# Routed attention and a squared-ReLU layer on one core: the last attention sums placed behind all remaining plain products

## The chip, the cores and the metric

The kernel runs on one core of a Trainium2 chip. The metric is the device time of one execution in microseconds (us); the figure for a kernel is the median of its runs. A profile is one further execution, recorded by the hardware profiler. The engines are called as the profile calls them: PE (TensorE matmuls), PEld (its weight loads), DVE (VectorE), ACT (ScalarE), POOL (GpSimd) and SP (SyncE, which issues most transfers here).

## What is computed

The reference has two halves. Attention with routing: queries and keys go to the nearest of 16 centroids, and a query sees only keys of its own cluster. Then a layer that squares its ReLU.

```python
# q, k, v: (4, 8, 768, 64); centroids: (8, 16, 64)
q_assign = argmax(q_n @ c_n)              # per head
k_assign = argmax(k_n @ c_n)
scores = (q @ k.T) / 8, or -1e9 where q_assign != k_assign
attn = softmax(scores);  attn_out = attn @ v
# x: (3072, 512), w_in: (512, 2048), w_out: (2048, 512)
x = attn_out, heads side by side
out = relu(x @ w_in) ** 2 @ w_out
```

## The kernel before

Attention runs in units: a pair of heads, a half of the queries, and two of six key chunks. The scores are exponentiated on ACT and masked on DVE. The products with v are summed on PE in a PSUM tile `av`. The sums for the softmax's denominator are first accumulated on POOL in `acc`, and then summed over partitions on PE (`sm`). `add_up` makes the reciprocal and sends it through DRAM to be spread over the partitions (`rb`); `finish` scales `av` with it into `xT`, the input of the second layer.

```python
def add_up(pair, h):                       # cut: the branch of the first pairs
    total = acc.pop((pair, h))
    sm = bank("sm", [P, TB // 2])
    one = [ones_products(sm, e, total[:, e], True, True) for e in range(2)]
    together([p for both in zip(*one) for p in both])      # four products on PE
    r = once.tile([P, TB // 2], F32, name="r")
    nc.vector.reciprocal(out=r, in_=sm)
    ...
    nc.sync.dma_start(far.rearrange("e (g n) -> (e g) n", g=2), r)
    for e in range(2):
        nc.sync.dma_start(rb[D * e : D * (e + 1)], far[e].partition_broadcast(D))
    nc.sync.dma_start(seen[row : row + 4], r)

def finish(pair, h):
    nc.vector.scalar_tensor_tensor(out=x, in0=av.pop((pair, h), x), scalar=UP,
        in1=spread_out.pop((pair, h)), op0=ALU.mult, op1=ALU.mult)
```

The second layer exists in two forms. The plain one, `ffn`, is used for the first of the four batches only. It is a generator whose products are dealt out among the attention units, so that PE has work where attention waits; `fill_steps(n)` takes the next products of it, up to n columns. `left[0]` is what remains of it, and the share of each unit is computed so that `RESERVE = 3 * DM` columns stay for the end.

```python
for u in range(len(units) + 3):
    ...                                    # scores, finish, products with v
    for pair, h in complete:
        with tc.high_priority(offset=1000) if first_half(pair, h) else ExitStack():
            add_up(pair, h)
    ...
    fill_steps(left[0] - goal)             # this unit's share of plain products
...
fill_steps(left[0])                        # what is left of them
ctx.close()                                # attention's buffers are given back
banks = fast.enter_context(tc.tile_pool(name="banks", bufs=8, space=PSUM, reuse_waits="tile"))
```

The other form, `ffn_pair`, does the remaining three batches after attention, with seven products of half size for eight (a Strassen-Winograd scheme). It needs sums of its inputs beforehand: of `xT` and of `w_out` on DVE (`x_t`, and `w_t` 1 to 4), of `w_in` on POOL (`w_s`). Its PSUM tiles, called `bank`, are eight, and lie where attention's PSUM tiles lay (`sc`, `av`, and `sm` with the others of its pool), so that a product into a bank waits for the last reader of what was there.

```python
def combine(c, product, width, early=()):  # cut
    product(1, bank); nc.scalar.copy(out=c11, in_=bank)
    add(6, (c12, c11)); add(2, (c11, c11)); add(7, (c21, c12))
    add(5, (c22, c21), (c12, c12)); sub(c21, c21, bank_of(4)); add(3, (c12, c12))

for i in range(F2):                        # first part of a batch, cut
    w_s = ...                              # s1..s4: four sums on POOL
    if i > 1 and w_sums:
        to, one, two = w_sums.pop(0)
        sub(w_t[to], one, two)             # sums of w_out on DVE
    combine(c, product, TB)                # products on PE, sums on DVE
```

The order of instructions on each engine is made by the scheduler from this program, its dependences and priorities.

Of the kernel before, what the change touches and what calls it, by code (L numbers as in the profile page):

```python
# [25 lines left out]
def kernel(  # L26
# [88 lines left out]
    def load_v(pair):  # L115
        b, hp = divmod(pair, HP)
        raw_v[pair] = loads_v.tile([P, 2, NCH, D], F32, name="v_raw")
        nc.sync.dma_start(
            raw_v[pair], v[b, 2 * hp : 2 * hp + 2].rearrange("h (p j) d -> p h j d", p=P)
        )  # L120
# [16 lines left out]
    def load_weights(i):  # L137
        raw_w[i] = wstage.tile([P, NW, 2], U32, name="w_raw")
        nc.sync.dma_start(raw_w[i], weights[i][1])
# [134 lines left out]
    def split_words(pair, which):  # L274
        if which == 0:
            words[pair] = dram.tile([2 * NCH, P, 2, 2 * D], U16, name="words")
        flat = loads.tile([P, NCH, 2, 2 * D], U16, name="flat", tag="qk")
        src = raw[pair][which].bitcast(U16).rearrange("p c (d two) -> p c two d", two=2)
        half = NCH // 2
        with tc.issue_after(last_exp[0]):  # L280
            for cols in (slice(0, half), slice(half, NCH)):
                nc.scalar.copy(out=flat[:, cols], in_=src[:, cols])
        nc.sync.dma_start(
            words[pair][NCH * which : NCH * (which + 1)].rearrange("c p two d -> p c two d"),
            flat,
        )
        if which == 1:
            raw.pop(pair)
            load_qk(pair + 1)
# [126 lines left out]
    def prep(pair):  # L416
        if pair < HP:
            return [
                lambda: turn(pair, 0), lambda: turn(pair, 1), lambda: turn(pair, 2),
                lambda: logits(pair), lambda: route(pair),  # L420
                lambda: turn_onehot(pair, 0), lambda: turn_onehot(pair, 1),
            ]

        split = [lambda i=i: split_words(pair + 1, i) for i in range(2 if pair + 1 < NG else 0)]
        first, second = split or (None, None)
        return [
            lambda: turn_words(pair), None, None, first, None, None,
            lambda: logits(pair), None, lambda: route(pair), second, None, None,
            None, None, lambda: spread(pair),
        ]  # L430
# [10 lines left out]
    def first_half(pair, h):  # L441
        return pair < HP and h == 0
# [62 lines left out]
    def times_v(pair, h, c):  # L505
        if c == 0:
            av[pair, h] = ps_av.tile([P, TB], F32, name="av", tag="av")
            if first_half(pair, h):
                sums[pair, h] = ps_av.tile([P, TB // 2], F32, name="sm", tag="av")
        t = ex.pop((pair, h, c))  # L510
        products = [
            dict(
                out=av[pair, h][D * e : D * (e + 1)], lhsT=raw_v[pair][:, e, c + i],
                rhs=t[:, 2 * i + e], start=(c + i == 0), stop=(c + i == NCH - 1),
            )
            for i in range(2) for e in range(2)
        ]
        if first_half(pair, h):
            for i in range(2):
                one = [  # L520
                    ones_products(
                        sums[pair, h], e, t[:, 2 * i + e], c + i == 0, c + i == NCH - 1
                    )
                    for e in range(2)
                ]
                products += [p for both in zip(*one) for p in both]
        together(products, 4000)
# [76 lines left out]
    def ffn_pair(pools, b):  # L604
# [114 lines left out]
    units = [  # L719
        (pair, h, c)  # L720
        for pairs, halves in [(range(HP), [0]), (range(HP), [1])]
        + [([pair], [0, 1]) for pair in range(HP, NG)]
        for pair in pairs for h in halves for c in range(0, NCH, 2)
    ]
# [3 lines left out]
    left = [len(PLAIN) * per_half]  # L728
# [11 lines left out]
    def fill_steps(columns):  # L740

        while fill and columns > 0:
            if (passed := next(fill[0], None)) is None:
                fill.pop(0)
            else:
                columns -= passed
                left[0] -= passed

    def behind_first(u, what=last_logits):
        return tc.issue_after(what[0]) if u == 0 else ExitStack()  # L750

    def next_pair(u):

        pair, h, c = units[u]
        if c == 0 and pair + 1 < NG and h == 0 and (pair + 1) not in qkT:
            if pair + 1 < HP or pair >= HP:
                return pair + 1
        if u == TWOS + 4:
            return HP
        return None  # L760
# [17 lines left out]
    def ends(halves):  # L778
        for pair, h in halves:
            b, hp = divmod(pair, HP)  # L780

            with tc.high_priority(offset=1000) if (pair, h) == (HP - 1, 0) else ExitStack():
                finish(pair, h)
            if hp == HP - 1 and (b, h) in PLAIN:
                fill.append(ffn(b, h))

    for u in range(len(units) + 3):
        if u < len(units):
            pair, h, c = units[u]
            if (p := next_pair(u)) is not None:  # L790
                ahead.extend(prep(p))
            if u in (TWOS, TWOS + 2):

                split_words(HP, int(u > TWOS))
            if c == 0 and u + 3 < len(units) and units[u + 3][0] not in raw_v:
                load_v(units[u + 3][0])

            with behind_first(u):
                scores(pair, h, c)

        ends(added)
        added.clear()
        if u < TWOS:
            ready = u - 1
        elif u == TWOS or u % 2 or u >= len(units):
            ready = u

        complete, late = late, []
        while v_next < min(ready, len(units)):
            pair, h, c = units[v_next]  # L810
            times_v(pair, h, c)
            v_next += 1
            if c == NCH - 2:
                (late if h and not HP * NCH <= u < len(units) else complete).append((pair, h))
        for pair, h in complete:
            with tc.high_priority(offset=1000) if first_half(pair, h) else ExitStack():
                add_up(pair, h)
            if h == 1:
                for d in (qkT, ids, qid):
                    d.pop(pair)  # L820
            if h == 1 or pair < HP:
                raw_v.pop(pair)
            added.append((pair, h))

        rounding += 4
        while rounding >= 3:
            rounding -= 3
            i = next(to_round, None)
            if i is not None:
                with tc.issue_after(last_exp[0]):  # L830
                    round_weights(i)
                if (i := next(loaded, None)) is not None:
                    load_weights(i)
            elif not later:
                early.close()
                for name, bufs in (("xT", 5), ("out", 2)):
                    later[name] = keep.enter_context(
                        tc.tile_pool(name=name + "_late", bufs=bufs, side="right",
                                     reuse_waits="tile")
                    )  # L840
        share = 0
        if u % 2 == 0 or not TWOS < u < len(units):
            n = 2 if TWOS < u < len(units) else 1
            share = max(0, left[0] - RESERVE) * sum(map(density, range(u, u + n)))
            share //= max(1, sum(map(density, range(u, ENDS))))
        goal = left[0] - share

        for i in range(3):
            if i == 2:
                fill_steps(share * 2 // 3)  # L850
            if ahead:
                with behind_first(u, masked if i else last_logits):
                    (ahead.pop(0) or int)()
        fill_steps(left[0] - goal)
# [235 lines left out]
```

## Time and profile before

| | |
|---|---|
| time, median of 3 runs | 976.93 us (975.26 to 977.56) |
| span of the profiled run | 979.1 us |
| DVE busy, 530 to 539 us | 7.18 of 9.00 us |
| PE busy, 530 to 539 us | 7.41 of 9.00 us |
| PE busy, 539 to 560 us | 21.00 of 21.00 us |
| PE busy, 560 to 974 us | 413.37 of 414.00 us |
| granted TensorE clock | 0.997 |

In the page, a row of digits cuts the span into 40 slices and gives the busy share of each in tenths. In the chain of waits, each line has a start, a duration and the instruction that the end of the run is traced back to. In the timeline a line has a start, a busy time, engine, line of the kernel, operation, output and inputs with shapes, the number of merged instructions, and in brackets how long the engine sat idle before it and which instruction ended that. Attention ends near 534 us; the rest of the span is the second layer of three batches. Plain products are called `po` in its second part; `bank` stands for the products of the last stage.

### The profile page before, as it was taken

Reading aid. Unit: us, or ns where it says so; the run is one execution under the profiler, and the core shown is the slowest. Engines: PE = TensorE matmul, PEld = TensorE weight load, DVE = VectorE, ACT = ScalarE, POOL = GpSimd, SP = SyncE. Lnnn points to the kernel's source line nnn. Section 1 sums busy time; section 2 is a strip of 40 time slices with the busy share of each in tenths; the row PEclk is TensorE's granted clock in tenths of the full one; section 3 lists DMA queues with packets and bytes.
Section 4 is the critical chain, followed back from the end, with each engine's and each line's share of the span. In section 5 each row is a group of like instructions: output and inputs, shape, how many; then the busy total and the mean of one; then the engine's idle time right before and its main releaser. Section 6 shows DMA issues by size and latency. Waiting matters only on the chain.

```text
span 979.1 us, 12064 instructions
## 1 busy us (share of the span) xinstructions
PE 959.3 (98%) x4479; PEld 552.6 (56%) x4479; DVE 563.5 (58%) x913; ACT 316.1 (32%) x511; POOL 381.1 (39%) x277
## 2 busy tenths in 40 slices
PE   8999999999999999999999999999999999999997
PEld 4544444433444444444343555888556888556886
DVE  4869666666566665665657966531556531656331
ACT  5887655444445555544331211000111000111000
POOL 1337766555656556565567431002231002231000
PEclk9999999999999999999999999999999999999999
DMA  9667671544545454452310000000000000000000
GB/s 249 187 198 201 195 196 51 127 116 107 136 110 138 118 125 113 108 142 67 82 42 12 20 1 0 12 25 27 3 1 1 22 22 21 1 1 0 22 22 25
DMA packets 127746, 74.54 MB, mean 76 GB/s; under 512 B 90944, under 2 KB 119104, under 8 KB 127680
## 3 DMA queue, kind: packets, MB, share of 16 engines
q1 hardware_dynamic: 125968, 73.26, 28.4%
q8 instruction: 38, 0.62, 0.3%
q10 hardware_dynamic: 1712, 0.43, 0.2%
q14 instruction: 28, 0.23, 0.1%
HBM read 48.27 MB, written 15.86 MB: 65 GB/s over the span
## 4 chain that ended last, share of the span: by engine, by line
PE 81%; issue 6%; DVE 4%; DMA 4%; POOL 3%; SPq 2%; ACT 0%; POOLq 0%; DVEq 0%; ACTq 0%
PE bank L701 22%; PE bank L670 22%; PE ph L578 7%; PE po L591 7%; PE sc L91 6%; PE sc L94 5%; PE av L91 5%; PE av L94 4%; POOL w_in L167 2%; DMA rb<-far_r 2%; PE sm L91 1%; DVE ex L478 1%; DVE w_raw L155 1%; PE lg L91 1%; DMA qid<-far 1%
## 5 line engine op out<-in xcount | busy, mean ns | idle before, releaser
L490 POOL TENSOR_TENSOR acc<-acc,ex 128x768 f32<-128x768 f32 x112 | 207.2, 1850 | 109.3 <-DVE ex L478 94.8
L478 DVE SCALAR_TENSOR_TENSOR ex<-qid,ids,sc 128x384 f32<-128x384 bf16 x288 | 157.8, 608 | 64.9 <-ACT sc L474 42.0
L474 ACT ACTIVATE sc<-sc 128x768 f32<-128x768 f32 x144 | 108.5, 792 | 160.9 <-PE sc L94 138.8
L94 PE MATMUL sc<-qkT 64*128 64x384 f32 x576 | 152.3, 503 | 0.8
L94 PE MATMUL av<-ex,v_raw 128*64 128x384 f32 x576 | 135.6, 491 | 0.0
L659 POOL TENSOR_TENSOR w_s<-w_in 128x256 f32<-128x256 f32 x24 | 18.2, 757 | 273.8 <-PE bank L701 162.0
L640 DVE TENSOR_TENSOR g<-bank,g 128x384 f32<-128x384 f32 x144 | 77.8, 556 | 79.0 <-PE bank L670 77.9
L578 PE MATMUL ph<-xT,w_in 128*128 128x384 f32 x256 | 93.0, 505 | 4.0 <-DVE r L545 2.3
L701 PE MATMUL bank<-w_out,g 128*128 128x256 f32 x432 | 95.2, 379 | 0.0
L591 PE MATMUL po<-w_out,gT 128*128 128x512 f32 x192 | 91.7, 609 | 0.0
L91 PE MATMUL sc<-qkT 64*128 64x384 f32 x192 | 87.1, 534 | 3.0 <-DVE ex L478 2.8
L701 PEld LDWEIGHTS bank<-w_out,g 128*128 128x128 f32 x432 | 82.1, 190 | 11.8
L640 DVE TENSOR_TENSOR osb<-bank,osb 128x256 f32<-128x256 f32 x54 | 22.1, 423 | 107.6 <-PE bank L701 102.2
L94 PEld LDWEIGHTS sc<-qkT 64*128 64x128 f32 x576 | 65.1, 186 | 27.9 <-issue 5.3
L91 PE MATMUL av<-ex,v_raw 128*64 128x384 f32 x192 | 80.4, 500 | 0.0
L488 POOL TENSOR_TENSOR acc<-ex 128x768 f32<-128x768 f32 x28 | 51.5, 1839 | 51.0 <-DVE ex L478 37.9
L578 PEld LDWEIGHTS ph<-xT,w_in 128*128 128x128 f32 x256 | 46.5, 192 | 43.6 <-issue 15.3
L670 PE MATMUL bank<-xT,w_in 128*128 128x384 f32 x192 | 69.9, 487 | 0.0
L670 PE MATMUL bank<-x_t,w_s 128*128 128x384 f32 x192 | 69.8, 486 | 0.0
L670 PE MATMUL bank<-xT,w_s 128*128 128x384 f32 x192 | 69.8, 486 | 0.0
L94 PEld LDWEIGHTS av<-ex,v_raw 128*64 128x64 f32 x576 | 49.5, 137 | 34.1 <-issue 34.0
L701 PE MATMUL bank<-w_t,g 128*128 128x256 f32 x288 | 65.1, 379 | 0.0
(127 smaller groups left out, 1224.5 us busy)
## 6 DMA issues: line engine op xcount, KB each, us to landing
words<-flat SPq DMA_DIRECT2D x24, 384.0 KB
w_raw<-in_moe_w_in_dram SPq DMA_DIRECT2D x16, 512.0 KB
w_raw<-in_moe_w_out_dram SPq DMA_DIRECT2D x16, 512.0 KB
v_raw<-in_v_dram SPq DMA_DIRECT2D x20, 384.0 KB
rb<-far_r SPq DMA_DIRECT2D x64, 96.0 KB
q_raw<-in_q_dram SPq DMA_DIRECT2D x31, 192.0 KB
k_raw<-in_k_dram SPq DMA_DIRECT2D x31, 192.0 KB
out_dram<-osb SPq DMA_DIRECT2D x23, 256.0 KB
```

Source lines behind the costliest of these rows:

```text
L91: last = nc.tensor.matmul(**next(products))
L94: last = nc.tensor.matmul(**product)
L167: nc.gpsimd.tensor_tensor(out=dst, in0=dst, in1=lo, op=ALU.add)
L474: last_exp[0] = nc.scalar.activation(out=t[:, 2 * i : 2 * i + 2] if pair < HP else src, in_=src, func=ACT.Exp, scale=SCALE).ins
L478: last_mask[0] = nc.vector.scalar_tensor_tensor(out=t[:, 2 * i + e], in0=qid[pair][1][:, h, e], scalar=ids[pair][:, ch % NB, 2 + ch // NB, ...
L488: nc.gpsimd.tensor_tensor(out=acc[pair, h], in0=t[:, 0:2], in1=t[:, 2:4], op=ALU.add)
L490: nc.gpsimd.tensor_tensor(out=acc[pair, h], in0=acc[pair, h], in1=t[:, 2 * i : 2 * i + 2], op=ALU.add)
L578: nc.tensor.matmul(ph, lhsT=w_in[:, kk, f * P : (f + 1) * P], rhs=xT[b, h][:, kk], start=(kk == 0), stop=(kk == KT - 1),)
L591: nc.tensor.matmul(po, lhsT=gT[f][:, i * P : (i + 1) * P], rhs=w_out[:, f], start=(f == 0), stop=(f == FT - 1),)
L640: nc.vector.tensor_tensor(out=out, in0=bank, in1=to, op=ALU.add)
L670: nc.tensor.matmul(bank, lhsT=operands[j][0][:, kk], rhs=operands[j][1][:, kk], start=(kk == 0), stop=(kk == H2 - 1),)
L701: nc.tensor.matmul(bank, lhsT=operands[j][0][:, f], rhs=operands[j][1][:, f], start=(f == 0), stop=(f == F2 - 1),)
```

## The change

One call is added in the loop over units. In the last two passes, after all units have been recorded (`u > len(units)`), all plain products that are left are recorded ahead of `add_up`, in place of after it. The aim is that PE has all seven of them to do while POOL still accumulates what the last sums need.

```diff
             if c == NCH - 2:
                 (late if h and not HP * NCH <= u < len(units) else complete).append((pair, h))
+        if u > len(units):
+
+            fill_steps(left[0])
         for pair, h in complete:
             with tc.high_priority(offset=1000) if first_half(pair, h) else ExitStack():
                 add_up(pair, h)
```

The order of the built program differs from there on as follows, engine by engine. PE: `po` x2, `sm` x4, `po` x5 becomes `po` x7, `sm` x4. DVE: the reciprocal, which stood before the first of the four sums of `w_out`, now stands after it; the `xT` of the last half head, which stood after the first of these sums, now stands after the fourth. SP: the output of the last plain product is issued ahead of the reciprocal's transfers, in place of behind them. POOL and ACT keep their order.

## The prediction

> **What bounds the kernel now.** I read the busy shares first, then the chain that ended last, then the timeline around 530 us, where the diff acts. The page's shares and slices:
>
> ```profile
> PE 959.3 (98%) x4479; PEld 552.6 (56%) x4479; DVE 563.5 (58%) x913; ACT 316.1 (32%) x511; POOL 381.1 (39%) x277
> ...
> PE   8999999999999999999999999999999999999997
> ```
>
> TensorE (PE) is busy 98% of the span, so time can change only where PE idles, or comes to idle. The end of the chain, from the trace:
>
> ```profile
> 528.83 2.39 POOL acc L490
> 531.22 0.04 issue
> 531.26 0.02 POOLq L659
> 531.28 0.02 issue
> 531.30 2.41 POOL acc L490
> 533.71 0.04 issue
> 533.75 0.35 PE sm L91
> ...
> 534.28 4.49 PE po L591 x10
> 538.77 72.24 PE bank L670 x224
> ```
>
> From 538.77 on PE works through the three last-stage blocks without a hole; the chain leaves it only for the tail at 973. So whatever the first of these products gains or loses is carried to the end, about one for one. The only PE hole near the diff is ahead of the last sums:
>
> ```profile
> 530.18 1.98 PE L591 MATMUL po<-w_out,gT 128*128 128x512 f32 x4
> 533.75 0.35 PE L91 MATMUL sm<-acc,ups 128*32 128x192 f32 x1 [1.59 <-POOL acc L490]
> ...
> 534.21 4.56 PE L591 MATMUL po<-w_out,gT 128*128 128x512 f32 x10
> 538.61 1.45 PE L670 MATMUL bank<-xT,w_in 128*128 128x384 f32 x4
> ```
>
> A float32 product leaves two records, so x4 is two plain products and x10 the other five. PE has only two to do while GpSimd (POOL) finishes its accumulation; 1.59 us are lost. VectorE (DVE) around it:
>
> ```profile
> 535.83 1.34 DVE L545 RECIPROCAL r<-sm 128x192 f32<-128x192 f32 x1
> ...
> 540.06 2.80 DVE L612 TENSOR_TENSOR w_t<-w_out 128x2048 f32<-128x2048 f32 x1
> 542.79 0.55 DVE L564 SCALAR_TENSOR_TENSOR xT<-av,rb 128x384 f32<-128x384 f32 x1
> 543.26 2.28 DVE L612 TENSOR_TENSOR w_t<-w_out,w_t 128x2048 f32<-128x2048 f32 x1
> 545.46 2.28 DVE L612 TENSOR_TENSOR w_t<-w_out 128x2048 f32<-128x2048 f32 x1
> ```
>
> The reader is to see the order: reciprocal, one weight sum, xT, then the other weight sums. The order decides the case.
>
> **What the Trainium skill says.** (1) "PSUM — Partial Sum Buffer", section "Engine vs sequencer instructions": the VectorE, ScalarE and GpSimd queues are strict first-in-first-out, and matmuls start in program order. So an instruction that stands behind a waiting one waits too. The trace agrees: the seven plain products depend on nothing from POOL, and five of them stand behind the sums until 533.75. (2) "SBUF — State Buffer", section "SBUF: two separate sides": a DVE operation with two SBUF inputs and a GpSimd operation that reads SBUF take one shared port pair in turn, each for its whole instruction. The trace agrees: at 548.12 a weight sum starts while a POOL operation of 0.72 us from 547.88 is under way, and shows 2.63 us in place of 2.28; the POOL operation queued behind it from 548.57 shows 2.78 us. From 529 to 537 the subtractions of DVE and the operations of POOL alternate one for one in this way.
>
> **The change part by part.** It adds no instruction and removes none: `fill_steps(left[0])` records all remaining plain products ahead of `add_up` of the last half head. [...] What moves on DVE follows from the scheduler. Before: subtractions, reciprocal, check of sums, w_t1, xT, w_t2, w_t3, first g sum, w_t4. After: subtractions, **w_t1, reciprocal, w_t2, w_t3, w_t4, xT**, check of sums, g sums.
>
> Two waits of the new program decide what this costs. The second bank product needs the PSUM bank of the last sums, so it waits for the reciprocal that reads them. The seventh needs the bank of the last av, so it waits for xT. Both waits are in the old program too, but were over when PE came (reciprocal at 537.17 against a product at 539.90; xT at 543.34 against 546.35).
>
> Now in steps, in times of this trace.
> - PE, gain. The seven products run through: 532.16, the end of the first two, plus 5 x 0.854 (two records of 0.427) is 536.43. GpSimd's accumulation is over by 533.7, so the sums follow without waiting, and the first bank product starts at 538.61 - 1.59 = 537.02. **-1.59.**
> - DVE, w_t1. In the built program it waits for the last plain product, so it can't start before 536.43. POOL's operation of 0.73 us from 536.46 has the port, until 537.15. A free weight sum takes 2.20 from start to start (543.26 to 545.46): end 539.3.
> - Reciprocal, 1.36 (its rows give 1.345 to 1.359): end 540.65, where it ended at 537.17.
> - The second bank product was due at 537.02 + 1.29 = 538.31. It starts at 540.7: **+2.4.**
> - w_t2, w_t3, w_t4: three times 2.20, and POOL has three of its eight early operations (0.7 each) still to do, taking the port between them: 540.65 + 6.6 + two such waits of 0.7 is 548.65. xT, with one operand in PSUM, adds 0.5: 549.1. Its data is there: rb landed some 5.2 us after the reciprocal in the occurrence before (520.85 to 526.03), which is 545.9 here.
> - The seventh product is due five products after the second, 540.7 + 5 x 1.29 = 547.15, and starts at 549.15: **+2.0.**
> - Sum: -1.59 + 2.4 + 2.0 = **+2.8 us.** After that I find no further wait. The first ScalarE copy also waits for xT and ends near 549.7; the check of sums and the g sums follow on DVE, the first bank is free before the ninth product (551.7), and later ones come free faster than PE takes them: ten operations of some 0.55 in 9.03 us of PE.
>
> If the port is free whenever DVE wants it, the same sum gives: reciprocal at 540.05, second product +1.8, xT at 547.15, seventh product +0.65, in all +0.85. The alternation seen from 529 to 537 speaks for the longer one.
>
> **The rivals.**
> 1. *The plain reading:* the hole is filled and nothing else happens, -1.6 us, about 975.3. For it: the hole is on the chain, and PE is full behind it. Against it: w_t1 now stands ahead of the reciprocal and three sums ahead of xT, and the PE waits name those two.
> 2. *Only the bank of the sums counts:* the seventh product finds xT done, since w_t2 to w_t4 run undisturbed or the weight sums are shorter than I take them. -1.59 + 2.4, about +0.8: 977.7.
> 3. *The transfer is the bound:* far_r, then rb, start 3.5 us later and share the queue with the 256 KB output of the plain product. If rb took 8.5 us in place of 5.2, xT would wait for it and the loss would grow past 2.8. The DMA share is near 0 there, which speaks against it.
> 4. *Hidden:* the stall is made up by slack later. Against it: PE shows 413.37 us busy of 414 from 560 to 974.
>
> **Range and chances.** The mechanism gives +0.85 to +2.8, and I lean to the upper part: +2.6 on 976.93 is 979.5. The runs of the kernel before spread by 2.3 us, so I take about 1.6 to either side: 977.9 to 981.1. A 2% change is 19.5 us; the whole transition, from the hole to the last weight sum, is about that long, so nothing here can reach it. Within 2%: 0.98; each other side 0.01.
>
> **What would show it.** In the changed profile: po x14 without a hole ahead of the sums, first bank product near 537.0; reciprocal ending near 540.6, with w_t directly ahead of it; PE waiting some 2.4 us at the second bank product for DVE r, and some 2 us at the seventh for DVE xT; all later products some 2 to 3 us later than before. If PE shows no wait at these two, rival 1 holds and the kernel is faster by 1.6. If only the first shows, rival 2. If DVE idles ahead of xT for rb, rival 3.

## The result, and the profile after

The changed kernel took 980.84 us (median of 6 runs, 979.16 to 982.31), the kernel before 976.72 beside it: a ratio of 1.0039, 95% interval 1.002 to 1.0058. A later comparison of the same two kernels gave 981.87 against 979.26, a ratio of 1.003 (1.0015 to 1.0045). The change makes the kernel slower by some 0.3%: it fills the hole of 1.59 us ahead of the last sums, and opens two behind them, of 2.35 and 1.39 us.

On the page of the changed kernel the shares look as before:

```profile
PE 958.0 (98%) x4479; PEld 551.6 (56%) x4479; DVE 564.2 (58%) x913; ACT 316.0 (32%) x511; POOL 387.0 (39%) x277
```

The difference lies in 20 us of the timeline. Shown are its lines of PE (start, busy time, engine, line, operation, count, and in brackets the idle time before it and what ended it):

```profile
528.57 6.28 PE L591 MATMUL po<-w_out,gT 128*128 128x512 f32 x14
...
535.24 1.56 PE L670 MATMUL bank<-xT,w_in 128*128 128x384 f32 x4
...
539.14 1.53 PE L670 MATMUL bank<-x_t,w_s 128*128 128x384 f32 x4 [2.35 <-DVE r L545]
...
544.38 1.45 PE L670 MATMUL bank<-x_t,w_in 128*128 128x384 f32 x4
...
547.22 1.53 PE L670 MATMUL bank<-xT,w_s 128*128 128x384 f32 x4 [1.39 <-POOL w_s L612]
548.58 1.45 PE L670 MATMUL bank<-xT,w_in 128*128 128x384 f32 x4
```

All fourteen records of the plain products run through, and the 1.59 us ahead of the sums are gone. The second bank product waits for the reciprocal, and the seventh waits too. DVE and POOL in the same stretch:

```profile
534.88 2.85 DVE L612 TENSOR_TENSOR w_t<-w_out 128x2048 f32<-128x2048 f32 x1 [0.57 <-PE po L591]
...
537.65 1.34 DVE L545 RECIPROCAL r<-sm 128x192 f32<-128x192 f32 x1
...
538.92 2.22 DVE L612 TENSOR_TENSOR w_t<-w_out,w_t 128x2048 f32<-128x2048 f32 x1
538.96 2.77 POOL L612 TENSOR_TENSOR w_s<-w_s,w_in 128x256 f32<-128x256 f32 x1
...
541.07 2.81 DVE L612 TENSOR_TENSOR w_t<-w_out 128x2048 f32<-128x2048 f32 x1
541.69 2.77 POOL L612 TENSOR_TENSOR w_s<-w_in 128x256 f32<-128x256 f32 x1
543.80 2.81 DVE L612 TENSOR_TENSOR w_t<-w_t,w_out 128x2048 f32<-128x2048 f32 x1
544.42 2.77 POOL L612 TENSOR_TENSOR w_s<-w_in,w_s 128x256 f32<-128x256 f32 x1
546.53 0.55 DVE L564 SCALAR_TENSOR_TENSOR xT<-av,rb 128x384 f32<-128x384 f32 x1
```

The weight sum w_t1 stands ahead of the reciprocal, the other three ahead of xT. DVE works without a pause from 534.88 until xT is done, and the two PE waits end 0.15 us behind the end of the reciprocal (538.99) and 0.14 us behind that of xT (547.08). For the second of them the profile names a POOL sum, which ends at 547.19; the experiments settle which of the two it was. Behind that nothing gives the time back. In the chain that ended last, PE is again one block to the end:

```profile
547.22 64.74 PE bank L670 x200
611.96 72.52 PE bank L701 x336
684.48 0.12 PE every L869 x2
684.60 72.44 PE bank L670 x224
```

Since attention starts and ends at slightly different times from run to run, I compare **stretches** within one profile, both from the start of the plain products behind the last av: A to the start of the eighth bank product, B to the product of the check of sums (`every`). The two ends in the kernel before, from its timeline and its chain:

```profile
547.64 1.45 PE L670 MATMUL bank<-xT,w_in 128*128 128x384 f32 x4
...
683.53 0.12 PE every L866 x2
```

Before: A is 547.64 - 530.18 = 17.46, B is 683.53 - 530.18 = 153.35. After: A is 20.01, B is 684.48 - 528.57 = 155.91. So the profile shows +2.56 us from the transition.

### The profile page after: what moved, and what is told of

It reads as the page before. It is cut to its first block, busy times and chain, and to the rows that moved or that the text cites. A ratio compares the mean times of both kernels' runs of the same rounds, so it can differ in the third digit from the quotient of the medians.

```text
span 980.0 us, 12063 instructions
## 1 busy us (share of the span) xinstructions
PE 958.0 (98%) x4479; PEld 551.6 (56%) x4479; DVE 564.2 (58%) x913; ACT 316.0 (32%) x511; POOL 387.0 (39%) x277
## 4 chain that ended last, share of the span: by engine, by line
PE 86%; DVE 4%; DMA 3%; ACT 2%; issue 2%; POOL 2%; SPq 1%; ACTq 0%; DVEq 0%; POOLq 0%
PE bank L701 22%; PE bank L670 21%; PE po L591 7%; PE ph L578 7%; PE sc L91 7%; PE sc L94 6%; PE av L91 6%; PE av L94 5%; PE sm L91 1%; DMA rb<-far_r 1%; DVE w_raw L155 1%; PE lg L91 1%; POOL w_s L612 1%; ACT ex L474 1%; DVE ex L478 1%
## 5 line engine op out<-in xcount | busy, mean ns | idle before, releaser
L659 POOL TENSOR_TENSOR w_s<-w_in 128x256 f32<-128x256 f32 x24 | 20.2, 841 | 270.5 <-PE bank L701 162.0
```

Source lines behind the costliest of these rows:

```text
L659: nc.gpsimd.tensor_tensor(out=s1, in0=a[1][0], in1=a[1][1], op=ALU.add)
```

## The experiments

My theory: the loss is DVE's order. Rivals: plain products ahead of the sums cost by themselves, or through their output's transfer, which is now issued ahead of the reciprocal's (rival B); the seventh product waits for the POOL sum that the profile names, not for xT (rival C). In the table, the ratio with its interval compares the runs of both kernels and is not the quotient of the two medians; for `four` it is 0.9998, the quotient 0.9986.

| kernel | A, us | B, us | median beside before's, us | ratio (95%) |
|---|---|---|---|---|
| before | 17.46 | 153.35 | | |
| changed | 20.01 | 155.91 | 980.84 / 976.72 | 1.0039 (1.002 to 1.0058) |
| again | 20.01 | 155.90 | 981.87 / 979.26 | 1.003 (1.0015 to 1.0045) |
| four | 15.80 | 152.77 | 977.93 / 979.26 | 0.9998 (0.9985 to 1.001) |
| both | 16.60 | 156.62 | 980.62 / 979.26 | 1.0016 (1.0004 to 1.0029) |
| sm_av | 20.02 | 157.60 | 984.84 / 979.26 | 1.0067 (1.0047 to 1.0087) |
| four_late | 15.80 | 151.69 | 977.63 / 978.84 | 0.9985 (0.9976 to 0.9995) |
| seven_late | 16.13 | 152.02 | 977.07 / 978.84 | 0.9988 (0.9974 to 1.0002) |

**Four products ahead (four).** The edit against the changed kernel:

```diff
-        if u > len(units):
+        if u == len(units) + 1:
-            fill_steps(left[0])
+            fill_steps(2 * DM)
```

> Two plain products more ahead of the last sums (four, then three behind them), in place of all seven. I measure a stretch in the profile, from the start of the plain products behind the last av to the start of the eighth bank product: 17.46 us before (530.18 to 547.64), 20.01 in the changed kernel (528.57 to 548.58). Theory A (the loss is the order on DVE: reciprocal behind w_t1, xT behind w_t2 to w_t4): here the last plain product ends behind the sums, w_t1 cannot pass the reciprocal, PE waits nowhere, and the stretch is 17.46 - 1.59 = about 15.9; time about 975.1. Rival B (the loss comes from plain products as such ahead of the sums, or from their output's transfer ahead of the reciprocal's): a part of the loss stays, stretch above 17.

A was 15.80, as expected: no wait in it. B was only 0.58 below the kernel before, not 1.6, and the times don't separate the two. The list of what PE waited for from 540 us on has one line, with the total, the count and the longest:

```profile
PE bank L670 <- DVE g L640: 0.8, 1, 0.8
```

So there is a third place where DVE's backlog bites: the sums into g also stand behind w_t, and here the tenth product waits for the first of them to free its bank. Stretch A alone misses that.

**Both reorderings (both).** Against the changed kernel; the lines that keep the reciprocal and the last xT in `last_r` and `last_x` are left out:

```diff
-                sub(w_t[to], one, two)
+                with tc.issue_after(last_r[0]) if to == 1 else tc.issue_after(last_x[0]): sub(w_t[to], one, two)
```

> All seven products ahead, as in the changed kernel, but on DVE w_t1 is held behind the reciprocal and w_t2 to w_t4 behind xT. Theory A: the wait of the second bank product goes from 2.35 us to near 0.15; xT follows its transfer, some 5.2 us behind the reciprocal, and in the built program it is the sixth product that waits for xT, for some 0.6; stretch about 16.5, time about 975.7. Rival B (transfer order): the transfer of rb takes longer than 6 us, the stretch stays near 20.

A was 16.60 against 16.5 expected, with the wait of the second product gone. The time was a miss: I expected some 1 us less than the kernel before (975.7 against 976.72), and it took 1.4 us more than the one beside it (980.62 against 979.26). PE and DVE of this kernel:

```profile
541.78 1.56 PE L670 MATMUL bank<-x_t,w_in 128*128 128x384 f32 x4 [0.21 <-DVE xT L564]
...
549.38 2.40 PE L670 MATMUL bank<-xT,w_in 128*128 128x384 f32 x4 [2.17 <-DVE g L640]
551.58 2.34 PE L670 MATMUL bank<-xT,w_s 128*128 128x384 f32 x4
```

```profile
541.17 0.56 DVE L564 SCALAR_TENSOR_TENSOR xT<-av,rb 128x384 f32<-128x384 f32 x1 [1.97 <-DMA rb<-far_r]
541.64 2.28 DVE L612 TENSOR_TENSOR w_t<-w_out,w_t 128x2048 f32<-128x2048 f32 x1
...
546.04 2.82 DVE L612 TENSOR_TENSOR w_t<-w_t,w_out 128x2048 f32<-128x2048 f32 x1
548.78 2.80 DVE L640 TENSOR_TENSOR g<-bank,g 128x384 f32<-128x384 f32 x5
```

The three sums that I put behind xT now lie ahead of the first g sum, which starts at 548.78, and PE, at the tenth product, stands for 2.17 us. The wait was moved, not removed. Of the 3.27 us that B is above the kernel before, 1.80 are another thing: the tenth and eleventh products took 2.20 and 2.18 us from start to start in place of 1.29, at a granted clock of 0.50. The profiled execution took 981.98 us, more than the median, so how often the clock falls here isn't shown.

**The last sums in another bank (sm_av).**

```diff
-            sm = bank("sm", [P, TB // 2])
+            sm = (ps_av.tile(..., name="sm", tag="av") if (pair, h) == (NG - 1, 1) else bank(...))
```

> As the changed kernel, but the last sums lie in the other PSUM buffer of av, so that the second bank product no longer takes the bank that the reciprocal reads. Order on all engines unchanged. If the two waits simply add (2.6 and 1.6 of them), the stretch falls from 20.01 to 17.4. Theory A in its sharper form: both waits hang on one chain of DVE, whose end is xT; the second product's wait vanishes, and the seventh's grows from some 1.5 to some 4.1, since xT ends where it did; stretch again 20.0, time as the changed kernel. Rival C (the seventh product waits for the POOL sum that the profile names): the same start of the seventh product, so this run doesn't tell that apart.

A was 20.02, as the sharper form expected: the first wait vanished and the second grew from 1.39 to 3.97 us. PE in a second profile of it:

```profile
536.16 1.45 PE L670 MATMUL bank<-x_t,w_s 128*128 128x384 f32 x4
...
546.74 2.89 PE L670 MATMUL bank<-xT,w_s 128*128 128x384 f32 x4 [3.97 <-POOL w_s L612]
549.43 1.82 PE L670 MATMUL bank<-xT,w_in 128*128 128x384 f32 x4
551.09 1.45 PE L670 MATMUL bank<-x_t,w_s 128*128 128x384 f32 x4
```

This shows that the second product waits because of the bank, and that in the changed kernel the end of xT alone sets stretch A; taking the first wait away buys nothing. The time was not the changed kernel's, but 3 us above again's. B, 1.69 above the changed kernel's, shows part of it: behind the long wait a product takes 2.7 us (546.74 to 549.43) in place of 1.29, at a granted clock of 0.50.

**The changed kernel again (again).**

> The changed kernel once more, unaltered, for the size of the loss beside the others of this call: theory A gives +2.5 us over the kernel before (stretch 20.0), where the first comparison gave +4.1 with an interval of 2.0 to 5.7. If +4 stands, some 1.5 us lie outside the stretch.

+2.6 us by the medians, and A and B to within 0.01 of the first profile.

**The weight sums later (four_late and seven_late).** Both hold each sum of w_out behind the last squaring on DVE of the group before, with four plain products ahead of the sums or all seven. The line that keeps the squaring in `squared` is left out:

```diff
-                sub(w_t[to], one, two)
+                with tc.issue_after(squared[0]): sub(w_t[to], one, two)
```

> Four plain products ahead of the sums and three behind, and the four sums of w_out on DVE held behind the first, second, third and fourth groups of bank products (they are needed some 70 us later). The runs so far showed that the stretch to the eighth product isn't all: where it was short, PE waited once more behind it, for the first g sums, which stand behind w_t on DVE. So I now measure from the start of the plain products behind the last av to the product of the check of sums: 153.35 us before, 155.91 in the changed kernel, 152.77 with four ahead alone, 156.62 with both reorderings. Theory A, amended: DVE's backlog of the w_t sums is the cause of all three waits. Then no wait is left here: 153.35 - 1.66 = 151.7, time about 1.6 us under the kernel before. If something else delays the g sums (the transfer of rb, xT), a wait of 0.5 us or more stays.

> The changed kernel with all seven plain products ahead, and only the w_t sums held back as in the run before this. Amended theory A: the change by itself gains; the second product waits some 0.3 us for the reciprocal, which follows the sums at once, and nothing else waits: 152.0, time about 1.3 us under the kernel before. Rival B (plain products ahead of the sums, or their output's transfer ahead of the reciprocal's, cost by themselves): 154 or more.

B was 151.69 and 152.02, and PE's list of waits behind 540 us is empty in both. In the kernel with all seven ahead, DVE reads:

```profile
533.05 1.36 DVE L545 RECIPROCAL r<-sm 128x192 f32<-128x192 f32 x1 [1.07 <-PE sm L94]
...
539.74 0.56 DVE L564 SCALAR_TENSOR_TENSOR xT<-av,rb 128x384 f32<-128x384 f32 x1 [2.72 <-DMA rb<-far_r]
540.97 2.81 DVE L640 TENSOR_TENSOR g<-bank,g 128x384 f32<-128x384 f32 x5 [0.67 <-ACT g L644]
```

With the weight sums out of the way, all seven products ahead give a B 1.33 us below the kernel before, and 3.89 below the changed kernel. That refutes rival B: the plain products are all ahead, and their output's transfer goes first here too; from the end of the reciprocal (534.41) to xT are 5.3 us, as between an earlier pair in the kernel before (5.2 us, 520.85 to 526.03). The kernel before with only its sums held back wasn't run; its PE has no wait behind the sums (21.00 us busy of 21.00 from 539 to 560), which leaves nothing there to gain. In the times, seven_late isn't separated from the kernel before (its interval contains 1). Four_late has the shorter B, and its interval lies below 1: it is 0.15% faster than the kernel before.

**POOL's sums held back (pool_late, three profiles).** A copy of two elements of xT on POOL stands ahead of the four sums for the second group. Of the edit only the copy is shown; the sums are ordered behind it:

```diff
+ behind = nc.gpsimd.tensor_copy(out=..., in_=xT[B - 1, 1][:, KT - 1, 0:2]).ins   # for (b, i) == (1, 1)
```

> The changed kernel, but the four POOL sums for the second group of bank products are held back by a copy of two elements that reads xT. Port theory: in the changed kernel the second and third of w_t2 to w_t4 show 2.81 us for 2.2 because POOL sums lie between them; without these, each takes 2.2 to 2.3, xT ends 1.1 us earlier, and the eighth product starts 18.9 us behind the first plain product in place of 20.0. If the seventh product waits for the POOL sum that the profile names in front of it (w_s, which now ends some 3 us behind xT), its start moves back to 21.5 or later instead. If DVE's durations don't depend on POOL, nothing moves: 20.0.

> The kernel with the held POOL sums once more, unaltered. Its first profile showed xT done 17.45 us behind the first plain product, against 18.51 in the changed kernel, but the eighth product at 20.1: behind the wait of 2.36 us for the reciprocal the granted clock stood at 0.50 for some 3.4 us, and two products took 2.13 and 2.22 us for 1.29. Clock theory: the drop depends on how the wait falls in time, not on the kernel. If it stays away here, the eighth product starts at 18.9. If the slow products come from the held POOL sums, they are there again at full clock.

> The same again, for one more drawing: 18.9 at full clock, or 20.1 with a drop to 0.50 behind the wait.

A was 20.10, 18.95 and 19.98, B 155.99, 154.84 and 155.88. Each is one execution, so its time isn't compared. The second profile had full clock in this stretch; DVE and PE in it:

```profile
538.03 2.22 DVE L612 TENSOR_TENSOR w_t<-w_out,w_t 128x2048 f32<-128x2048 f32 x1
540.18 2.27 DVE L612 TENSOR_TENSOR w_t<-w_out 128x2048 f32<-128x2048 f32 x1
542.37 2.28 DVE L612 TENSOR_TENSOR w_t<-w_t,w_out 128x2048 f32<-128x2048 f32 x1
```

```profile
545.26 1.53 PE L670 MATMUL bank<-xT,w_s 128*128 128x384 f32 x4 [0.32 <-DVE xT L564]
546.63 1.45 PE L670 MATMUL bank<-xT,w_in 128*128 128x384 f32 x4
```

The second and third of these sums take 2.27 and 2.28 us in place of 2.81, xT ends 1.1 us earlier, and the seventh product follows xT. So POOL's sums between them, which the prediction puts down to the shared port, cost 1.06 us of the loss (20.01 to 18.95). And rival C falls: the POOL sum that stood in brackets is now behind xT, and the product doesn't wait for it; in the changed kernel it ended 0.11 us behind xT. The other two profiles lost the gain to the clock. In the lines of the third, each stretch has the busy time of PE, PEld, DVE, ACT and POOL, and at the end the granted clock, the DMA share and GB/s:

```profile
535.00:536.00 1.00, 0.69 (x1) 0.50 (x2) 1.00 (x2) 0.00 (x0) 0.00 (x0) 0.56 0.00 0
536.00:537.00 1.00, 1.00 (x3) 0.61 (x2) 1.00 (x1) 0.00 (x0) 0.00 (x0) 0.50 0.02 5
537.00:538.00 1.00, 1.00 (x2) 0.40 (x2) 1.00 (x2) 0.00 (x0) 0.00 (x0) 0.50 0.00 1
538.00:539.00 1.00, 1.00 (x4) 0.61 (x3) 1.00 (x1) 0.00 (x0) 0.00 (x0) 0.73 0.54 126
```

**Two more profiles, for the clock (sm_av_2, again_2).**

> The kernel with the last sums in the buffer of av once more. There the two waits are one of 3.97 us, and the first profile showed the clock at 0.50 for some 3.4 us behind it. Clock theory: a longer wait is followed by the drop more often than one of 2.35 us; I expect it again, and the product of the check of sums near 157.6 us behind the first plain product. Without the drop: 155.9.

> The changed kernel a third time. In two profiles the clock stayed at 1.00 behind its waits (2.35 and 1.39 us) and the product of the check of sums stood at 155.9. If the drop can follow these too, it shows here with some luck, and adds 1.7.

B was 157.59 in sm_av_2, again with the clock at 0.50 behind the wait, and 155.89 in again_2, again without that.

## Why the prediction was right

The time fell inside the range, the direction was right, and the waits came where the text put them. In us behind the first plain product:

| step | predicted | measured |
|---|---|---|
| first bank product | 6.84 | 6.67 |
| end of the reciprocal | 10.47 | 10.42 |
| second bank product | 10.52 | 10.57 |
| end of xT | 18.92 | 18.51 |
| seventh bank product | 18.97 | 18.65 |
| sum against the kernel before | +2.8 | +2.56 |

- Gain: -1.76 in place of -1.59. The first wait delayed the second product by 2.61 in place of 2.4, the second wait the seventh by 1.63 in place of 2.0. These misses partly cancel, so the sum is closer than its terms.
- Port: I took two waits of 0.7 between w_t2 and w_t4; they were 0.59 each (2.81 against 2.22). pool_late shows that they are POOL's doing, and the alternation seen from 529 to 537 was the right guide.
- Rivals 1 to 3 fall: both waits are there, DVE doesn't idle ahead of xT for rb, and the seventh product waits for xT as foretold, although the profile names a POOL sum; pool_late settled that. Rival 4 falls too: PE shows 414.00 us busy of 414 from 560 to 974.
- "After that I find no further wait" holds for the changed kernel, but only because PE is late anyway. In `four` and `both` the g sums behind w_t make a wait of their own.
- What misleads is the form of the sum, +2.4 and +2.0 as two costs. sm_av shows one: where xT ends on DVE. Taking the first wait away made the second longer by 2.58.
- Luck: of the +4.1 us of the first comparison the profile explains 2.56; the second comparison gave 2.6. The rest lies inside the first interval (2.0 to 5.7 us) and isn't shown to be the change's. The range was also tied to the level of 976.93: in the second comparison both kernels were slower, and 981.87 lies outside it. The difference was foretold well, the absolute time with some luck.

## What to carry to other kernels

When work is moved ahead on the engine that bounds, look at what it releases on the others: here the built order put a weight sum that waits for the last plain product ahead of the reciprocal that PE waits for, although PE first reads such a sum at 618.70, 72 us behind the last of the four. Work that isn't urgent has to be held back by an order of its own; here that turned +2.56 us of B into -1.33. And when two waits of one engine hang on the same chain of another, shortening the first need not shorten the whole: find the last link.

## What the runs showed of the hardware

A wait of PE of some 2 us can be followed by half clock. In the transition, behind a wait of 2.17 us (both), of 2.35 us (pool_late, two of three profiles) and of 3.97 us (sm_av, both profiles) the granted clock stood at 0.50 for 3.4 us, which cost 1.7 to 1.8 us of B where no later wait took it up. Behind the 2.35 us of the changed kernel it stayed at 1.00 in three profiles of three. Near 100 us, in attention, seven of the 13 profiles have such a wait too, of 1.92 to 2.63 us, and five of them the same drop behind it. In the kernel before:

```profile
101.82 8.41 PE L578 MATMUL ph<-xT,w_in 128*128 128x384 f32 x20 [2.35 <-DVE r L545]
...
104.00:105.00 1.00, 1.00 (x3) 0.65 (x2) 0.96 (x2) 0.00 (x0) 0.92 (x2) 0.50 1.17 247
```

The Trainium skill, "TensorE: Matmul & The Clock Gate", section "Part 1: The HAM clock gate (the "warmup" mystery)", gives half clock after at least one idle window of some 3.4 us, and says that this window is free-running, so that the point of a change depends on where in it a kernel's first product falls. That one and the same wait is followed by the drop in some profiles only would fit such a window; no run here shows the window itself. The waits of 2.07 to 2.63 us that were followed by the drop are shorter than the 3.4 us, so in this case a wait need not be that long. How the chance depends on its length these profiles don't settle.
